# Lightning attention and an FNet block on one core: the late pairs' second layer as 49 block products instead of 7 half-size ones

## The chip, the cores and the metric

The kernel runs on one core of one Trainium2 chip. A core has a matrix engine (TensorE, in the profile PE, its weight loads PEld), a vector engine (VectorE, DVE), a scalar engine (ScalarE, ACT), a general one (GpSimd, POOL) and an engine that issues DMAs (SyncE, SP). Each takes its instructions in order from its own queue, and they wait for each other through semaphores. The metric is the device time of one execution in microseconds, as the median of several runs.

## The reference

Attention with a decaying state (4 batches, 8 heads, 768 positions, 64 wide), then an FNet block over the result, seen as x of 4 x 768 x 512. What the change touches is the last part, a two-layer network applied to each row:

```python
X = np.fft.fft(x, axis=1)
X = np.fft.fft(X, axis=2)
u = x + np.real(X)
un = (u - mean(u)) / np.sqrt(var(u) + 1e-06)
ch = np.maximum(un @ w_ch1, 0.0) @ w_ch2     # 512 -> 2048 -> 512
return u + ch
```

All data are float32.

## The kernel before

**Stages.** Attention of a batch runs by chunks of 128 positions (attn, L270 to L353), its Fourier transform and normalisation (fft_ln, L414 to L612) follow. The rows of a batch are 6 tiles of 128 x 512, taken two at a time: 12 groups (b, g), of G = 2 tiles each. The first four are PLAIN: their two layers (mlp, L636 for the first and L650 for the second) are woven into attention and transforms of later batches, so that TensorE always has something to do. The other eight are LATE. For them fft_ln writes the transposed normalised rows (utd) and the rows themselves (ud) to HBM, and after everything else they are done in four pairs by late(j), called for j = 0 to 3.

**A late pair.** One pair is a product of two matrices cut into 2 x 2 blocks, done by the Strassen-Winograd scheme: 7 block products instead of 8, on sums of blocks. The sums of weight blocks are made once, by combine_weights, part 0 before the end of the plain work and part 1 after it (w1s, w2s, and in place in w1 and w2). Late(j) first makes sums of the input blocks on DVE (L713 to L716), then the first layer: for each of HF = 8 blocks of 128 hidden columns, seven products of two matmuls each (prod, L723). ACT and DVE take the results out of PSUM, add what the scheme adds, apply the ReLU and make the sums that the second layer needs as stationary operands: h tiles named a11, a12, a22, s1, s2, s3, s4 (ha.. and hs.. in the profile). Finish(i) does the end of block i while block i+1 has begun.

The second layer (prod2, L770) runs for each of the two tiles s: seven products, each 8 matmuls of 128 x 256 that accumulate over the hidden dimension in one PSUM bank. The banks X, Y and Z are chained: the scheme's running sums are accumulated in X and Z, and DVE reads X after each step, adding the residual rows (u2, loaded by SP from ud) into the output tile y2. Store writes a tile to the output: tiles of the first half of the sequence by SP (L623), mirrored ones by an indirect DMA on GpSimd's queue (L625).

**What sets the order.** The program is written in Python generators that are woven by estimated times. The framework then orders the instructions of each engine by its own estimate, except where keep_in_program_order pins them; the order on each queue is fixed when the kernel is built. Pools reuse memory: the pools of the late part (h2, y2, p2) open when the plain ones close, on the same addresses, and "reuse_waits='tile'" makes the first use of a new tile wait for all that used its memory before.

**Memory, where it matters below.** The plain pools lie at the right-hand end of SBUF, one behind the other, per partition: x (12 tiles of 2 KB), ut (3 of 4 KB), y (one tile of 2 KB), hr (4 of 4 KB). When they are closed the pool h2 takes the same place, its tiles in the order of their first use.

Of the kernel before, what the change touches and what calls it, by code (L numbers as in the profile page):

```python
# [76 lines left out]
def kernel(  # L77
# [602 lines left out]
    def combine_weights(part):  # L680
# [16 lines left out]
        for o, x, y, op in todo:  # L697
            n = o.shape[1]
            for i in range(0, n, n // 2):
                V.tensor_tensor(o[:, i:i + n // 2], x[:, i:i + n // 2], y[:, i:i + n // 2], op=op)  # L700
                yield 1.3

    def load_u(j, queue=nc.sync):

        r = s2.u[j] = new(s2.up, [128, 2, KO, G * 128], "ur", bufs=2)
        for h, (b, g) in enumerate(LATE[2 * j:2 * j + 2]):
            queue.dma_start(r[:, h], utd[b, g])

    def late(j):
        r = s2.u.pop(j)  # L710
        b11, b21, b12, b22 = r[:, 0, 0:2], r[:, 0, 2:4], r[:, 1, 0:2], r[:, 1, 2:4]
        t = new(s2.up, [128, 3, 2, G * 128], "us")
        V.tensor_tensor(t[:, 0], b12, b11, op=SUB)  # L713
        V.tensor_tensor(t[:, 1], b22, t[:, 0], op=SUB)
        V.tensor_tensor(t[:, 2], b21, t[:, 1], op=SUB)
        V.tensor_tensor(b12, b22, b12, op=SUB)  # L716
        U = dict(b11=b11, b21=b21, b22=b22, t1=t[:, 0], t2=t[:, 1], t4=t[:, 2], t3=b12)

        h = {n: new(s2.hp, [128, G, HF, 128], f"h{n}") for n in ("a11", "a12", "a22", "s1", "s2", "s3", "s4")}
# [12 lines left out]
        def finish(i, X, Z):  # L732
            a11, a12, a22, s1, s2_, s3, s4 = (h[n][:, :, i, :] for n in ("a11", "a12", "a22", "s1", "s2", "s3", "s4"))
# [7 lines left out]
            V.tensor_tensor(s2_, s1, a11, op=SUB)  # L741
            V.tensor_tensor(s3, a11, a21, op=SUB)
            V.tensor_tensor(s4, a12, s2_, op=SUB)

        last = None
        for i in range(HF):
# [16 lines left out]
            last = (i, X, Z)  # L763
        finish(*last)
        if 2 * j + 2 < len(LATE):
            load_u(j + 1)

        def prod2(ps, a, b, s, first):
            for i in range(HF):
                nc.tensor.matmul(ps, lhsT=h[a][:, s, i, :], rhs=s2.B[b][:, i, :],  # L770
                                 start=(first and i == 0), stop=(i == HF - 1), skip_group_check=True)

        lo, hi = slice(0, HM), slice(HM, DM)
        for s in reversed(range(G)):
            who = [(b, TT[g][s]) for b, g in LATE[2 * j:2 * j + 2]]
            us, y = [], []
            for k in who:
                us.append(new(s2.yp, [128, DM], "u2", bufs=3))
                nc.sync.dma_start(us[-1], ud[k])
                y.append(new(s2.yp, [128, DM], "y2", bufs=2))  # L780
            rev = slice(DM - 1, HM - 1, -1)
            X, Y, Z = bank(), bank(), bank()
            prod2(X, "a11", "b11", s, True)
            V.tensor_tensor(y[0][:, lo], X, us[0][:, lo], op=ADD)
            prod2(Y, "a12", "b21", s, True)
            V.tensor_tensor(y[0][:, lo], Y, y[0][:, lo], op=ADD)
            prod2(X, "s2", "t2", s, False)
            V.tensor_tensor(y[1][:, lo], X, us[1][:, lo], op=ADD)
            prod2(Z, "s3", "t3", s, True)
            prod2(X, "s1", "t1", s, False)  # L790
            V.tensor_tensor(y[1][:, hi], X, us[1][:, rev], op=ADD)  # L791
            V.tensor_tensor(y[1][:, hi], Z, y[1][:, hi], op=ADD)
            if s == 0:
                store(*who[1], y[1], hi)
            prod2(X, "s4", "b22", s, False)
            V.tensor_tensor(y[0][:, hi], X, us[0][:, rev], op=ADD)  # L796
            store(*who[0], y[0])
            prod2(Z, "a22", "t4", s, False)
            V.tensor_tensor(y[1][:, lo], Z, y[1][:, lo], op=ADD)
            store(*who[1], y[1], lo if s == 0 else slice(0, DM))  # L800


# [103 lines left out]
```

## Time and profile before

| what | value |
|---|---|
| time, median of 3 runs | 822.02 us (821.09 to 824.20) |
| span of the profiled execution | 819.4 us |
| end of the plain work, start of the late pairs | 428.3 us |
| first layer of one late pair (L723) | 48.35 us |
| second layer of one late pair (L770) | 48.35 us |
| records of L770 (two for each float32 matmul) | 896 |
| last TensorE work to the end of the span | 3.5 us |
| mean granted TensorE clock | 1.000 |

The span runs from the first to the last instruction of one profiled execution; the page has no separate time for that execution, and the timed runs lie 1.7 to 4.8 us above its span. A row of the costliest groups gives a line, an engine, what is written from what, the shape, the count, busy time and mean duration of one. Two groups of GpSimd that the working below uses, from the groups by form:

```profile
L270 POOL TENSOR_TENSOR kd<-k,decay 128x512 f32<-128x512 f32 x20 | 23.0, 1152 | 94.8 <-PE pa L315 64.5 <-DMA k<-in_k_dram 16.8 <-issue 10.3
L319 POOL TENSOR_TENSOR st<-st,qpow 128x256 f32<-128x256 f32 x16 | 15.9, 996 | 34.7 <-PE pa L328 24.3 <-DVE st L320 5.3 <-PE pa L332 2.8
```

The means include waiting; the shortest are 1.06 and 0.62 us. A float32 matmul appears as two MATMUL records and two LDWEIGHTS records; [...]the distance between starts (216 ns in the second layer) is what it costs.

### The profile page before, as it was taken

Reading aid. Unit: us, or ns where it says so; the run is one execution under the profiler, and the core shown is the slowest. Engines: PE = TensorE matmul, PEld = TensorE weight load, DVE = VectorE, ACT = ScalarE, POOL = GpSimd, SP = SyncE. Lnnn points to the kernel's source line nnn. Section 1 sums busy time; section 2 is a strip of 40 time slices with the busy share of each in tenths; the row PEclk is TensorE's granted clock in tenths of the full one; section 3 lists DMA queues with packets and bytes.
Section 4 is the critical chain, followed back from the end, with each engine's and each line's share of the span. In section 5 each row is a group of like instructions: output and inputs, shape, how many; then the busy total and the mean of one; then the engine's idle time right before and its main releaser. Section 6 shows DMA issues by size and latency. Waiting matters only on the chain.

```text
span 819.4 us, 11694 instructions
## 1 busy us (share of the span) xinstructions
PE 795.2 (97%) x4608; PEld 634.9 (77%) x4608; DVE 437.8 (53%) x1018; ACT 186.5 (23%) x448; POOL 86.1 (11%) x102
## 2 busy tenths in 40 slices
PE   6989899999999999999999999999999999999998
PEld 5777767768585857768648888888888888888886
DVE  5899798766743761354895541165313661146311
ACT  3756344225420211312002200022001210022100
POOL 3223340011011010220000000000000000000000
PEclk9999999999999999999999999999999999999999
DMA  9979624248741136530351011100111001010010
GB/s 233 249 154 271 174 90 129 63 113 201 203 125 51 52 62 131 129 123 26 93 162 42 1 53 51 52 1 1 64 40 52 0 1 39 33 33 0 1 39 26
DMA packets 126684, 68.88 MB, mean 84 GB/s; under 512 B 111150, under 2 KB 112174, under 8 KB 126630
## 3 DMA queue, kind: packets, MB, share of 16 engines
q1 hardware_dynamic: 121488, 55.67, 26.6%
q0 software_dynamic: 2112, 6.69, 2.4%
q10 hardware_dynamic: 3030, 5.78, 1.9%
q8 instruction: 36, 0.59, 0.3%
q14 instruction: 18, 0.15, 0.1%
HBM read 48.72 MB, written 19.40 MB: 83 GB/s over the span
## 4 chain that ended last, share of the span: by engine, by line
PE 80%; DVE 10%; issue 4%; DMA 3%; ACT 2%; POOL 1%; POOLq 0%; ACTq 0%; DVEq 0%
PE p L770 24%; PE p L723 24%; PE pm L650 10%; PE pm L636 8%; PE pa L332 3%; PE pa L516 3%; PE pa L298 3%; DMA x<-xb,ix 2%; PE pa L328 2%; PE pa L274 1%; DVE sc L302 1%; PE pa L315 1%; PE pa L348 1%; PE pa L279 1%; DVE stt L546 1%
## 5 line engine op out<-in xcount | busy, mean ns | idle before, releaser
L636 PE MATMUL pm<-ut,w 128*128 128x256 f32 x512 | 119.2, 382 | 0.0
L650 PE MATMUL pm<-w,hr 128*128 128x512 f32 x256 | 115.8, 597 | 0.2 <-DVE w L225 0.2
L636 PEld LDWEIGHTS pm<-ut,w 128*128 128x128 f32 x512 | 94.4, 190 | 15.4 <-issue 3.6
L723 PE MATMUL p<-ur,w 128*128 128x256 f32 x384 | 93.8, 379 | 0.0
L650 PEld LDWEIGHTS pm<-w,hr 128*128 128x128 f32 x256 | 46.6, 190 | 49.5 <-issue 48.0
L723 PEld LDWEIGHTS p<-ur,w 128*128 128x128 f32 x384 | 73.0, 190 | 10.3 <-issue 0.5
L723 PE MATMUL p<-us,w1s 128*128 128x256 f32 x256 | 65.7, 379 | 0.0
L770 PE MATMUL p<-w,hs 128*128 128x256 f32 x256 | 58.0, 379 | 0.5 <-DVE y L791 0.5
L770 PE MATMUL p<-w2s,hs 128*128 128x256 f32 x256 | 57.9, 379 | 0.0
L770 PE MATMUL p<-w,ha 128*128 128x256 f32 x256 | 57.9, 379 | 0.0
L770 PEld LDWEIGHTS p<-w,hs 128*128 128x128 f32 x256 | 48.5, 190 | 7.5 <-DVE y L791 0.9
L625 POOL DMA_INDIRECT out_dram<-y,ix x12 | 11.9, 989 | 402.6 <-DVE y L796 342.6
L770 PEld LDWEIGHTS p<-w2s,hs 128*128 128x128 f32 x256 | 48.6, 190 | 6.6
L723 PEld LDWEIGHTS p<-us,w1s 128*128 128x128 f32 x256 | 48.6, 190 | 6.6
L770 PEld LDWEIGHTS p<-w,ha 128*128 128x128 f32 x256 | 48.6, 190 | 6.6
L750 ACT COPY ha<-p 128x256 f32<-128x256 f32 x32 | 11.9, 372 | 169.1 <-PE p L723 139.4
L761 DVE TENSOR_TENSOR ha<-p,ha 128x256 f32<-128x256 f32 x32 | 13.6, 424 | 45.2 <-ACT ha L760 45.2
L298 PEld LDWEIGHTS pa<-qT,kT 64*128 64x128 f32 x384 | 26.0, 193 | 13.2 <-ACT qT L281 7.3
L302 DVE TENSOR_TENSOR sc<-pa,decay 128x512 f32<-128x512 f32 x48 | 31.5, 683 | 8.8 <-PE pa L298 8.5
L332 PE MATMUL pa<-sc,v 128*64 128x128 f32 x384 | 32.1, 284 | 4.1 <-DVE sc L302 4.1
L298 PE MATMUL pa<-qT,kT 64*128 64x128 f32 x384 | 30.7, 292 | 3.2 <-ACT qT L281 2.9
L270 POOL TENSOR_TENSOR kd<-k,decay 128x512 f32<-128x512 f32 x20 | 23.0, 1152 | 94.8 <-PE pa L315 64.5
(144 smaller groups left out, 1135.0 us busy)
## 6 DMA issues: line engine op xcount, KB each, us to landing
raw<-in_moe_w_ch_dram SPq DMA_DIRECT2D x32, 512.0 KB, 4.8
k<-in_k_dram SPq DMA_DIRECT2D x24, 256.0 KB, 5.0
q<-in_q_dram SPq DMA_DIRECT2D x24, 256.0 KB, 5.9
v<-in_v_dram SPq DMA_DIRECT2D x24, 256.0 KB, 4.9
ud<-x SPq DMA_DIRECT2D x16, 256.0 KB, 2.3
utd<-e SPq DMA_DIRECT2D x64, 64.0 KB, 2.2
u<-ud SPq DMA_DIRECT2D x16, 256.0 KB, 2.7
ur<-utd SPq DMA_DIRECT2D x6, 512.0 KB, 4.3
```

The source lines that it names most:

```text
L270: nc.gpsimd.tensor_tensor(kd, kt, kpow, op=ALU.mult)
L298: mm(pss[hi][:, hp, :], lhsT=kT[HD[hi], hp, :], rhs=qT[HD[hi], hp, :], start=True, stop=True)
L302: nc.vector.tensor_tensor(t, pss[hi], decay[:, hi::2, :], op=ALU.mult)
L328: mm(po[HD[hi], hp, :], lhsT=s_old[HD[hi], hp, :], rhs=qs[HD[hi], hp, :], start=(hp == 0), stop=False, skip_group_check=True)
L332: mm(po[HD[hi], hp, :], lhsT=vt[:, 2 * hp + hi, :], rhs=sc[hi][:, hp, :], start=(c == 0 and hp == 0), stop=(hp == HP - 1), skip_group_chec ...
L516: mm = nc.tensor.matmul(ps[0:m, n, :], lhsT=piece(a, i, n), rhs=cs[0:rows, a, i in (2, 3), n, :], start=(a == 0), stop=(a == 1))
L625: nc.gpsimd.indirect_dma_start(out=out.rearrange("b s d -> (b s) d"), out_offset=row_of(2 + HC * (b + 1) + T - HC), in_=y[:, :], in_offset ...
L636: nc.tensor.matmul(ps, lhsT=w1[:, c, 128 * fc:128 * fc + 128], rhs=ut[:, c, :], start=(c == 0), stop=(c == KO - 1))
L650: nc.tensor.matmul(ps, lhsT=hr[(fc - f0) // 4][:, fc % 4, 128 * i:128 * i + 128], rhs=w2[:, fc, :], start=(fc == f0), stop=(fc == f1 - 1))
L723: nc.tensor.matmul(ps, lhsT=s2.A[a][:, kt, 128 * i:128 * i + 128], rhs=U[b][:, kt, :], start=(first and kt == 0), stop=(kt == 1), skip_gro ...
L761: V.tensor_tensor(a22, two(Z), a22, op=ADD)
L770: nc.tensor.matmul(ps, lhsT=h[a][:, s, i, :], rhs=s2.B[b][:, i, :], start=(first and i == 0), stop=(i == HF - 1), skip_group_check=True)
```

## The change

The seven block products of the second layer are each cut once more by the same scheme, into seven products of quarter blocks: 49 instead of 56. Now both tiles of a group take part (the two tiles are the row halves of the second level), so the loop over s is gone, and a matmul is 128 x 128 with 4 steps of accumulation.

- **Stationary side.** S1, S2 and S4 of a product are sums of quarters of an h tile, made on DVE (prepare_a) into tiles "sx"; the third one is made in place (split). The h tiles s2 and s4 are no longer made in the first layer: they come in the second, in place of a11 and a12, half on DVE and half on GpSimd (part_sum).
- **Moving side.** T1, T2 and T4 of a weight block are made on GpSimd for each product of each pair (prepare_b) into tiles "tx", two sets; the fourth sum is made once, in place, by seven GpSimd instructions at the end of combine_weights(1).
- **Results.** Level2 runs one product: seven groups of four matmuls, a bank read after each (give): by ACT for the first write of a fresh quarter, else by DVE, which adds. Two products are interleaved, the preparation of the next one beside them. What the outer scheme adds between outputs is done on DVE (after), the residual is added on GpSimd (add_u).
- **Tiles.** y2 now holds the whole pair, ur has one buffer instead of two, and the input sums t1, t2, t4 use the "sx" tiles.

The diff, cut:

```diff
@@ -699,24 +699,68 @@
             for i in range(0, n, n // 2):
                 V.tensor_tensor(o[:, i:i + n // 2], x[:, i:i + n // 2], y[:, i:i + n // 2], op=op)
                 yield 1.3
+        if part:
+            for b in s2.B.values():
+                q = quarters_b(b)
+                nc.gpsimd.tensor_tensor(q[1], q[3], q[1], op=SUB)
+    def quarters_a(t):
+        return [t[:, s, i:i + HF // 2] for s in range(2) for i in (0, HF // 2)]
+    def quarters_b(t):
+        return [t[:, i:i + HF // 2, m:m + HM // 2] for i in (0, HF // 2) for m in (0, HM // 2)]
 
     def load_u(j, queue=nc.sync):
 
-        r = s2.u[j] = new(s2.up, [128, 2, KO, G * 128], "ur", bufs=2)
+        r = s2.u[j] = new(s2.up, [128, 2, KO, G * 128], "ur")
         for h, (b, g) in enumerate(LATE[2 * j:2 * j + 2]):
             queue.dma_start(r[:, h], utd[b, g])
+    PRODUCTS = [("a11", "b11"), ("a12", "b21"), ("s3", "t3"), ("s2", "t2"), ("s4", "b22"), ("s1", "t1"), ("a22", "t4")]
 
     def late(j):
         r = s2.u.pop(j)
         b11, b21, b12, b22 = r[:, 0, 0:2], r[:, 0, 2:4], r[:, 1, 0:2], r[:, 1, 2:4]
-        t = new(s2.up, [128, 3, 2, G * 128], "us")
-        V.tensor_tensor(t[:, 0], b12, b11, op=SUB)
-        V.tensor_tensor(t[:, 1], b22, t[:, 0], op=SUB)
-        V.tensor_tensor(t[:, 2], b21, t[:, 1], op=SUB)
+        t1, t2, t4 = (new(s2.hp, [128, 2, G * 128], "sx", bufs=7) for _ in range(3))
+        V.tensor_tensor(t1, b12, b11, op=SUB)
+        V.tensor_tensor(t2, b22, t1, op=SUB)
+        V.tensor_tensor(t4, b21, t2, op=SUB)
         V.tensor_tensor(b12, b22, b12, op=SUB)
-        U = dict(b11=b11, b21=b21, b22=b22, t1=t[:, 0], t2=t[:, 1], t4=t[:, 2], t3=b12)
-
-        h = {n: new(s2.hp, [128, G, HF, 128], f"h{n}") for n in ("a11", "a12", "a22", "s1", "s2", "s3", "s4")}
+        U = dict(b11=b11, b21=b21, b22=b22, t1=t1, t2=t2, t4=t4, t3=b12)
+        h = {n: new(s2.hp, [128, G, HF, 128], f"h{n}") for n in ("a11", "a12", "a22", "s1", "s3")}
+        pre_a, pre_b = {}, {}
+        def split(t):
+            A11, _, A21, _ = quarters_a(t)
+            V.tensor_tensor(A21, A11, A21, op=SUB)
+        def prepare_a(k):
+            a = PRODUCTS[k][0]
+            A11, A12, A3, A22 = quarters_a(h[a])
+            S1, S2, S4 = pre_a[k] = [new(s2.hp, [128, HF // 2, 128], "sx", bufs=7) for _ in range(3)]
+            if a in ("a11", "a12", "a22", "s3"):
+                split(h[a])
+                yield 0.0
+            V.tensor_tensor(S2, A22, A3, op=SUB)
+            yield 0.0
+            V.tensor_tensor(S1, S2, A11, op=ADD)
+            yield 0.0
+            V.tensor_tensor(S4, A12, S2, op=SUB)
+            yield 0.0
+        def prepare_b(k):
+            B11, T3, B21, B22 = quarters_b(s2.B[PRODUCTS[k][1]])
+            T1, T2, T4 = pre_b[k] = [new(s2.yp, [128, HF // 2, HM // 2], "tx", bufs=6) for _ in range(3)]
+            for o, x, y, op in ((T2, T3, B11, ADD), (T1, B22, T2, SUB), (T4, B21, T2, SUB)):
+                nc.gpsimd.tensor_tensor(o, x, y, op=op)
+                yield 0.0
 
         def prod(ps, a, b, i, first):
             for kt in range(2):
@@ -730,7 +774,7 @@
             return new(s2.ps, [128, DM], "p2")[:, 0:G * 128]
 
         def finish(i, X, Z):
-            a11, a12, a22, s1, s2_, s3, s4 = (h[n][:, :, i, :] for n in ("a11", "a12", "a22", "s1", "s2", "s3", "s4"))
+            a11, a12, a22, s1, s3 = (h[n][:, :, i, :] for n in ("a11", "a12", "a22", "s1", "s3"))
             prod(X, "s4", "b22", i, False)
             a21 = new(s2.hp, [128, G, 128], "a21", bufs=2)
             nc.scalar.activation(a21, two(X), AF.Relu)
@@ -738,9 +782,7 @@
             V.tensor_tensor(a12, two(Z), a12, op=ADD)
             V.tensor_scalar(a12, a12, 0.0, None, op0=ALU.max)
             V.tensor_tensor(s1, a21, a22, op=ADD)
-            V.tensor_tensor(s2_, s1, a11, op=SUB)
             V.tensor_tensor(s3, a11, a21, op=SUB)
-            V.tensor_tensor(s4, a12, s2_, op=SUB)
 
         last = None
         for i in range(HF):
@@ -761,44 +803,132 @@
             V.tensor_tensor(a22, two(Z), a22, op=ADD)
             V.tensor_scalar(a22, a22, 0.0, None, op0=ALU.max)
             last = (i, X, Z)
+            if i == HF // 2:
+                for k in range(2):
+                    run(prepare_b(k))
+        run(prepare_a(0))
         finish(*last)
+        run(prepare_a(1))
         if 2 * j + 2 < len(LATE):
             load_u(j + 1)
 
-        def prod2(ps, a, b, s, first):
-            for i in range(HF):
-                nc.tensor.matmul(ps, lhsT=h[a][:, s, i, :], rhs=s2.B[b][:, i, :],
-                                 start=(first and i == 0), stop=(i == HF - 1), skip_group_check=True)
-
-        lo, hi = slice(0, HM), slice(HM, DM)
-        for s in reversed(range(G)):
-            who = [(b, TT[g][s]) for b, g in LATE[2 * j:2 * j + 2]]
-            us, y = [], []
-            for k in who:
-                us.append(new(s2.yp, [128, DM], "u2", bufs=3))
-                nc.sync.dma_start(us[-1], ud[k])
-                y.append(new(s2.yp, [128, DM], "y2", bufs=2))
-            rev = slice(DM - 1, HM - 1, -1)
-            X, Y, Z = bank(), bank(), bank()
...
-            prod2(Z, "a22", "t4", s, False)
-            V.tensor_tensor(y[1][:, lo], Z, y[1][:, lo], op=ADD)
-            store(*who[1], y[1], lo if s == 0 else slice(0, DM))
-
+        who = [[(b, TT[g][s]) for s in range(G)] for b, g in LATE[2 * j:2 * j + 2]]
+        us = []
+        for k in who:
+            us.append(new(s2.yp, [128, G, DM], "u2", bufs=2))
+            for s in range(G):
+                nc.sync.dma_start(us[-1][:, s], ud[k[s]])
+        yt = new(s2.yp, [128, 2, G, DM], "y2")
+        T = new(s2.yp, [128, G, HM], "t2")
+        y11, y12, y21, y22 = (yt[:, k, :, m:m + HM] for k in range(2) for m in (0, HM))
+        def add_u(k, m, y):
+            u = us[k][:, :, 0:HM] if m == 0 else us[k][:, :, DM - 1:HM - 1:-1]
+            nc.gpsimd.tensor_tensor(y, y, u, op=ADD)
+        def part_sum(o, x, y, op):
+            V.tensor_tensor(o[:, 0], x[:, 0], y[:, 0], op=op)
+            nc.gpsimd.tensor_tensor(o[:, 1], x[:, 1], y[:, 1], op=op)
+        def stores(k, cols=slice(0, DM)):
+            for s in reversed(range(G)):
+                store(*who[k][s], yt[:, k, s], cols if s == 0 else slice(0, DM))
+        def after(k):
+            if k == 0:
+                split(h["s1"])
+                h["s2"] = h["a11"]
+                part_sum(h["a11"], h["s1"], h["a11"], SUB)
+            elif k == 1:
+                V.tensor_tensor(y11, y11, T, op=ADD)
+                h["s4"] = h["a12"]
+                part_sum(h["a12"], h["a12"], h["s2"], SUB)
+                add_u(0, 0, y11)
+            elif k == 3:
+                V.tensor_tensor(y21, T, y22, op=ADD)
+                add_u(1, 0, y21)
+                add_u(1, 1, y22)
+            elif k == 4:
+                add_u(0, 1, y12)
+            elif k == 5:
+                V.tensor_tensor(y12, y12, T, op=ADD)
+                stores(0)
+                V.tensor_tensor(y22, y22, T, op=ADD)
+                store(*who[1][0], yt[:, 1, 0], slice(HM, DM))
+            elif k == 6:
+                stores(1, slice(0, HM))
+        outs = [(T, True), (y11, True), (y22, True), (T, False), (y12, True), (T, False), (y21, False)]
+        def level2(k):
+            (a, b), (y, fresh) = PRODUCTS[k], outs[k]
+            A11, A12, A3, A22 = quarters_a(h[a])
+            B11, T3, B21, B22 = quarters_b(s2.B[b])
+            (S1, S2, S4), (T1, T2, T4) = pre_a.pop(k), pre_b.pop(k)
+            X, Y, Z = (bank()[:, 0:HM // 2] for _ in range(3))
+            def prod(ps, a, b, first):
+                for i in range(HF // 2):
+                    nc.tensor.matmul(ps, lhsT=a[:, i, :], rhs=b[:, i, :], start=(first and i == 0),
+                                     stop=(i == HF // 2 - 1), skip_group_check=True)
+            def give(ps, s, m, first=False):
+                o = y[:, s, m * HM // 2:(m + 1) * HM // 2]
+                if first and fresh:
+                    nc.scalar.copy(o, ps)
+                else:
+                    V.tensor_tensor(o, ps, o, op=ADD)
+            prod(X, A11, B11, True)
+            give(X, 0, 0, True)
+            yield 0.0
+            prod(Y, A12, B21, True)
+            give(Y, 0, 0)
+            yield 0.0
+            prod(X, S2, T2, False)
+            give(X, 1, 0, True)
+            yield 0.0
+            prod(Z, A3, T3, True)
+            give(Z, 1, 1, True)
+            yield 0.0
+            prod(X, S1, T1, False)
+            give(X, 1, 1)
+            yield 0.0
+            prod(Z, A22, T4, False)
+            give(Z, 1, 0)
+            yield 0.0
+            prod(X, S4, B22, False)
+            give(X, 0, 1, True)
+            yield 0.0
+            after(k)
+        n = len(PRODUCTS)
+        live = {}
+        for at in range(7 * n + 8):
+            k = at // 7
+            if at % 7 == 0 and k < n:
+                live[k] = level2(k)
+                if k + 1 < n and k:
+                    live[-k - 1] = turns(prepare_b(k + 1), prepare_a(k + 1))
+            for q in sorted(live, key=abs):
+                if q < 0 or (at - 7 * q) % 2 == 0:
+                    if next(live[q], live) is live:
+                        del live[q]
...
```

What is left out at the end is turns(), which takes steps of two generators by turns; in the removed loop it is the five products between the first line and the last.

More of the change, by code (lines that the diff above doesn't have):

```diff
@@ L773, in late @@
-        lo, hi = slice(0, HM), slice(HM, DM)
-        for s in reversed(range(G)):
-            who = [(b, TT[g][s]) for b, g in LATE[2 * j:2 * j + 2]]
-            us, y = [], []
-            for k in who:
-                us.append(new(s2.yp, [128, DM], "u2", bufs=3))
-                nc.sync.dma_start(us[-1], ud[k])
-                y.append(new(s2.yp, [128, DM], "y2", bufs=2))
-            rev = slice(DM - 1, HM - 1, -1)
-            X, Y, Z = bank(), bank(), bank()
[L783 to L797, printed above, removed]
-            prod2(Z, "a22", "t4", s, False)
-            V.tensor_tensor(y[1][:, lo], Z, y[1][:, lo], op=ADD)
-            store(*who[1], y[1], lo if s == 0 else slice(0, DM))
@@ new lines, in late, with turns @@
+        n = len(PRODUCTS)
[10 more added lines that the diff above has]
+                        del live[q]
+    def turns(*gens):
+        gens = list(gens)
+        while gens:
+            for g in list(gens):
+                d = next(g, None)
+                if d is None:
+                    gens.remove(g)
+                else:
+                    yield d
```

## The prediction

> **What bounds the kernel now.** I read the page first, then the chain of waits, then busy time by stage, then single instructions.
>
> ```profile
> PE 795.2 (97%) x4608; PEld 634.9 (77%) x4608; DVE 437.8 (53%) x1018; ACT 186.5 (23%) x448; POOL 86.1 (11%) x102
> PE   6989899999999999999999999999999999999998
> POOL 3223340011011010220000000000000000000000
> ```
>
> TensorE is busy 97% of the span and GpSimd is empty in its second half. The chain of waits from 428.3 us on is TensorE alone:
>
> ```profile
> 428.30 46.62 PE p L723 x216
> 475.78 1.73 PE p L723 x8
> 477.51 40.58 PE p L770 x188
> 518.95 6.91 PE p L770 x32
> 525.85 45.76 PE p L723 x212
> ```
>
> L723 is the first layer of a late pair, L770 the second; four rounds follow, each half lasting 48.35 us, with no wait between. Only TensorE time counts here, unless another engine becomes late. Busy time by stage shows how idle the others are:
>
> ```profile
> 477.50:525.85 48.35, 48.35 (x226) 42.56 (x225) 9.44 (x23) 0.37 (x1) 1.92 (x2) 1.00 0.19 63
> ```
>
> (columns: window, length, busy PE, PEld, DVE, ACT, POOL.) In a second layer DVE works 9.4 us, ACT 0.4, POOL 1.9. The change spends this idleness.
>
> **The change, part by part.**
>
> **1. Fewer multiplications.** Before: 2 x 7 x 8 = 112 matmuls of 128x256 (two records each) in 48.35 us, 0.432 us each. After: 49 x 4 = 196 matmuls of 128x128. Will one cost half? The weight load stays 128x128 and shows 190 ns per record, longer than half of 216. The timeline has a dense run of this shape in the Fourier stage:
>
> ```profile
> 274.55 0.39 PE L531 MATMUL pa<-dt,ys 128*128 128x129 f32 x2
> 274.67 0.30 PEld L532 LDWEIGHTS pa<-dt,ys 128*128 128x128 f32 x2
> 274.77 0.39 PE L532 MATMUL pa<-dt,ys 128*128 128x128 f32 x2
> 275.00 0.39 PE L534 MATMUL pa<-dt,ys 128*128 128x128 f32 x2
> ```
>
> Starts are 0.222 us apart with fresh weights each time; the loads overlap. The Trainium skill, "TensorE: Matmul & The Clock Gate" (LDWEIGHTS), gives columns/1.2 ns, 107 ns for 128; twice that is 0.213, just under. So 196 x 0.222 = 43.5 us, a gain of 4.85 a pair, **19.4 in all**. Ends: 0.213 gives 41.7, 0.23 gives 45.1 us.
>
> **2. New work on DVE and GpSimd.** Within one second layer (a pair):
> - DVE, both inputs in SBUF, 128x512: 18 sums for products 1 to 6, 4 output sums, 4 of the next pair's input sums (these move into this stage): 26 at a pitch of 0.60 (0.68 long); two 1024-wide at 1.14. Together 17.9 us. 33 additions out of PSUM (128x128): the rows at 128x256 have a pitch of 0.335, so about 0.20, 6.6 us. (16 copies go to ACT, about 0.28 each by L595: covered.) DVE: 24.5 of 43.5 us. The first layer loses 16 DVE sums and gains 8; it has 48.35 - 27 us free, so nothing.
> - GpSimd: 15 block sums of 128x512 (the other 6 fall into the first layer), two of 1024, 4 residual sums. L270 (128x512) takes 1.06 when undisturbed, L319 (128x256) 0.62, so 1024 about 1.9: 15 x 1.06 + 3.9 + 4.2 = 24 us. Both rows have a broadcast operand; the Trainium skill, "GPSIMD Engine Reference" (3.1), gives 4497 ns for 2048 fp32 elements, 1.1 to 1.2 for 512. I take 1.06; 1.2 for the range.
>
> Each fits alone. Together they may not: the Trainium skill, "SBUF — State Buffer" (Who interferes with whom), says that a DVE instruction with two SBUF inputs and a GpSimd one that reads SBUF share a port and block each other wholly. The trace agrees:
>
> ```profile
> 53.92 0.68 DVE L426 TENSOR_TENSOR fe<-x,x 128x512 f32<-128x512 f32 x1
> 54.08 2.27 POOL L319 TENSOR_TENSOR st<-st,qpow 128x256 f32<-128x256 f32 x1
> 55.46 0.41 DVE L430 TENSOR_TENSOR fo<-fo 128x255 f32<-128x255 f32 x1
> ...
> 83.12 1.55 POOL L270 TENSOR_TENSOR kd<-k,decay 128x512 f32<-128x512 f32 x1 [6.20 <-PE pa L315]
> ...
> 84.00 1.21 DVE L225 SCALAR_TENSOR_TENSOR w<-w,e 128x512 f32<-128x512 f32 x1
> ```
>
> L319 waits through four DVE sums and ends 0.5 after the last; L225 takes 1.21 for 0.72, ending 0.54 after L270. So 17.9 + 24 = 42 us of port in 43.5.
>
> **3. Stalls that follow.** A PSUM bank is reused four times in a product, three group times (4 matmuls, 0.888 us) after it was written: DVE may be 2.7 us late, then TensorE stops. DVE is in order, so an addition out of PSUM stands behind each waiting sum. From the instruction order of the changed kernel (fixed when it is built), counting from the start of the second layer:
> - GpSimd can begin T4 of product 2 only when TensorE has used the buffer (8th group, 7.1). Then come the half of s2, three sums of product 3, the half of s4: 4 x 1.06 + 2 x 1.9 = 8.1, with DVE's port time between them (about 3.5) until 18.7. DVE's first sum of product 4 waits for it; behind it stand two more sums and the addition that frees product 3's bank: 18.7 + 3 x 0.65 + 0.4 = 21, wanted at 19.5: **1.5 to 1.7**. (Without contention 0.2.)
> - DVE's S2 of product 6 reuses a buffer read in group 34; behind it S1, an output sum and the addition that frees group 37's bank: 0.1 + 3 x 0.6 + 0.2 + 0.35 = 2.45 against 1.78: **0.7**.
> - The next pair's second input sum reuses a buffer read in group 41, with one more sum and an addition ahead of group 43: 1.65 against 0.89, **0.8**, to 1.2 with GpSimd on the port; absent in the last pair.
> - The last groups of product 6, with two output sums among them: **0.5**.
>
> That is 3.9 a pair, 2.9 in the last: 14.6. Ends: 1.5 a pair (6) if GpSimd slips into DVE's gaps; 6.5 a pair (26) if sums take 1.2 and the two engines alternate throughout.
>
> **4. The hand-over at 428 us.** Nothing in the diff says it, the order does. GpSimd now makes 7 in-place differences and 6 block sums, and the store of the last plain tile (y, L625), which stood alone there, comes behind these 13. The new tiles "sx" (7 x 2 KB) come first in their pool and push ha22 to 30-38 KB; y lay at 36-38 (12 x 2 KB of x, 3 x 4 KB of ut below it). So the first ACT copy into ha22 waits for that store to land. Before, y lay under s2, which is written late and no longer exists. From the timeline of before:
>
> ```profile
> 429.52 1.08 POOL L625 DMA_INDIRECT out_dram<-y,ix  x1 [25.50 <-DVE y L662]
> 432.65 0.37 ACT L760 COPY ha<-p 128x256 f32<-128x256 f32 x1 [1.35 <-PE p L723]
> 434.18 1.03 PE L723 MATMUL p<-ur,w1s 128*128 128x256 f32 x4
> ```
>
> L760 is that copy; the matmuls at 434.18 need it, and all of ACT stands behind it. On GpSimd the first two differences can run at 418 to 421; then DVE's unbroken 1024-wide sums hold the port until 426.8. From there 11 sums of 1.06 plus about 2 us lost to DVE's input sums end at 440.4; issue to landing is 3.0 (the DMA issues' median): 443.4; copy and start of the matmul 0.6: 444 instead of 434.2, **9.8**. Least: two differences need the last plain matmul (428.3): 8 sums, 3.0, 0.6 give 440.4, so 6.2. Most, at 1.2 a sum: 12. The first pair's own input sums, now behind the last plain addition, come 2 us later; inside this stall.
>
> **5. Small things.** A load of the first late pair (512 KB) moves ahead of the mirror's write on ACT's queue, and the y store ahead of the two last gathers on GpSimd: the gather comes 2 us later (y is ready at 361.5, the gather was issued at 360.8). TensorE's order has more L636 work in front of L516 now, and before waited 1.0 there: +0.3, ends 0 and 2. SP: the next pair's load waits for the first layer's end, but no store is behind it that is ready. The tail: last additions are half as wide, but an indirect store ends it too: -0.3.
>
> **Sum.** -19.4 + 14.6 + 9.8 + 0.3 - 0.3 = +5.0 on the span of 819.4, which is 2.6 under the median of the timed runs: 824.4 + 2.6 = **827**.
>
> **Rivals.**
> - Not slower (the other side): GpSimd's sums fall into DVE's gaps. GpSimd has a lead of 6 to 12 us on most tiles, which speaks for it. Stalls 1.5 a pair, hand-over 7: 822 - 19.4 + 6 + 7 = **815.5**. It decides from a stall under 2.3 a pair with the hand-over as taken.
> - The port decides: sums at 1.2, alternating; a second layer of 43.5 + 6.5 = 50. 822 - 19.4 + 26 + 12 = **841**. For it: 42 of 43.5 us of port already; against: both engines also have work without it.
> - The store does not hold ACT (the wait is met early), stalls as forecast: 822 - 19.4 + 14.6 = **817**. Against: the copy's list of waits names that store's queue event.
>
> **How the numbers follow.** Forecast 0.48 (own range 821 to 833), not slower 0.26, port 0.18, store free 0.08. About 0.5% (4.1 us) is what a measurement tells from no change: bounds 817.9 and 826.1. Faster: 0.22 from the first rival and 0.05 from the third, 0.27. Same: the forecast's lower part 0.18, the rest of those two 0.07: 0.25. Slower 0.48. For 8 in 10: 812 to 841.
>
> **What would show it.** Right: in the changed trace TensorE idle for 6 to 12 us near 434 to 444, released by ACT's copy into ha22 and a store landing near 443; second layers of 46 to 48 us; stretched sums on POOL and DVE; matmul starts 0.222 apart. Wrong: a pitch above 0.23 for 128x128 (step 1), second layers near 44 (step 3), or no idle time near 434 (step 4).

## The result and the profile after

| what | before | after |
|---|---|---|
| time, median (4 runs each, side by side) | 823.06 us | 848.38 us |
| ratio after to before, 95% interval | | 1.0313 (1.0286 to 1.0340) |
| span of the profiled execution | 819.4 us | 844.8 us |
| second layer of a late pair, first matmul to first matmul of what follows | 48.35 us | 49.3 us (49.9 with its six early records) |
| last addition to the end of the span | 3.1 us | 9.9 us |

The change makes the kernel 3.1% slower, 25.3 us. 827 was forecast, with a range up to 841. The busy times and the slices of the page, after:

```profile
PE 787.0 (93%) x5280; PEld 645.1 (76%) x5280; DVE 581.3 (69%) x1158; ACT 203.1 (24%) x512; POOL 282.2 (33%) x217
PE   7989899999999999999978998999899998999995
POOL 3223240111111101210180059800894029910593
PEclk9999999999999999999989999999999999999998
```

TensorE is busy 8 us less than before (795.2), and yet the span is longer: the busy share fell from 97 to 93%. GpSimd, empty in the second half before, now has a burst at the start of the late part and four more at 80 to 90%, one for each second layer. The clock row, all nines before, has an 8 where the late pairs begin, and one at the end.

The chain of waits in the first second layer (start, length, engine and line), which was TensorE alone before:

```profile
492.06 4.70 PE p L875 x42
496.89 3.97 POOL tx L762 x2
500.86 2.76 POOL ha L832
503.62 2.22 POOL tx L762
...
507.47 1.71 POOL tx L762
509.17 2.77 POOL ha L832
...
515.26 8.29 PE p L875 x72
```

From 497 to 512 us the chain runs over GpSimd: the path that sets the end has moved to an engine that was to work beside it. A GpSimd sum of 128x512 takes 1.6 to 2.3 us there, where the working had 1.06.

TensorE's stops in this second layer, from the timeline of its matmuls (in brackets the idle time before a group, and what ended it):

```profile
499.99 1.16 PE L875 MATMUL p<-w,sx 128*128 128x128 f32 x8 [0.56 <-DVE t L883]
508.30 1.16 PE L875 MATMUL p<-w,sx 128*128 128x128 f32 x8 [1.79 <-DVE y L883]
515.26 1.13 PE L875 MATMUL p<-tx,sx 128*128 128x128 f32 x8 [1.33 <-DVE t L883]
533.99 1.13 PE L875 MATMUL p<-tx,hs 128*128 128x128 f32 x8 [0.63 <-DVE t L883]
540.17 1.16 PE L875 MATMUL p<-w2s,sx 128*128 128x128 f32 x8 [0.45 <-DVE y L883]
```

Each is ended by L883, DVE's addition out of PSUM that frees a bank. None is ended by GpSimd directly. What stands ahead of the addition, around the longest stop:

```profile
505.91 3.26 POOL L762 TENSOR_TENSOR tx<-w2s,tx 128x512 f32<-128x512 f32 x2
506.85 1.20 DVE L752 TENSOR_TENSOR sx<-sx,ha 128x512 f32<-128x512 f32 x1 [0.47 <-PE p L875]
507.97 0.28 DVE L883 TENSOR_TENSOR y<-p,y 128x128 f32<-128x128 f32 x1
508.17 1.55 DVE L754 TENSOR_TENSOR sx<-ha,sx 128x512 f32<-128x512 f32 x1
```

The addition takes 0.28 us, but waits its turn behind sums of 1.2 to 1.7 us that take 0.68 undisturbed. Before the second line DVE also stood 0.47 us for matmuls that had to end; by the program this can be the tile sx that it writes, which is not shown. The stops with the slower restarts behind them come to 6.2 us a pair: the same groups follow each other every 0.893 us elsewhere, and 49 x 0.893 = 43.8 against 49.9, both rounded. They repeat within 0.02 us in the second and third pair; the last, without a next pair's input sums, has the first three, 4.5 us.

The hand-over from the plain work to the late pairs:

```profile
430.59 4.61 POOL L705 TENSOR_TENSOR w<-w 128x512 f32<-128x512 f32 x3 [3.43 <-DVE w L700]
434.22 2.04 PE L767 MATMUL p<-sx,w1s 128*128 128x256 f32 x4 [1.80 <-DVE sx L728]
443.77 1.08 POOL L625 DMA_INDIRECT out_dram<-y,ix  x1 [0.17 <-issue]
446.83 0.37 ACT L802 COPY ha<-p 128x256 f32<-128x256 f32 x1 [10.16 <-DMA out_dram<-y,ix]
447.26 2.08 PE L767 MATMUL p<-ur,w1s 128*128 128x256 f32 x4 [5.59 <-ACT ha L802]
```

This is the stop of step 4: the store is issued at 443.8, ACT has been held for 10.2 us when it lands, and the matmuls that stood at 434.18 stand at 447.26. Two things are new: TensorE stops for 1.80 us at 434.22, for an input sum of DVE, and its clock falls. The four records at 434.22 and at 447.26 take 2.04 and 2.08 us, where four take 1.03 elsewhere: the granted clock is 0.50 from 433.3 to 440.1 and again from 446.9 to 450.3.

The end:

```profile
832.44 1.37 POOL L625 DMA_INDIRECT out_dram<-y,ix  x1 [4.02 <-DVE y L883]
834.65 0.29 DVE L883 TENSOR_TENSOR y<-p,y 128x128 f32<-128x128 f32 x1 [0.60 <-PE p L875]
835.65 6.48 SPq L623 DMA_DIRECT2D out_dram<-y  x3
838.92 0.97 POOL L625 DMA_INDIRECT out_dram<-y,ix  x1 [5.10 <-DMA out_dram<-y]
```

The last addition is done at 834.94, the span ends at 844.8. SP's stores begin when the first indirect store has landed (832.44 + 3.16 by the chain), the second indirect store when SP's have, and the last of SP's three when that one has.

### The profile page after: what moved, and what is told of

Same layout as the page of the kernel before. It is cut to its first block, busy times and chain, and to the rows that moved or that the text cites. A ratio compares the mean times of both kernels' runs of the same rounds, so it can differ in the third digit from the quotient of the medians.

```text
span 844.8 us, 13570 instructions
## 1 busy us (share of the span) xinstructions
PE 787.0 (93%) x5280; PEld 645.1 (76%) x5280; DVE 581.3 (69%) x1158; ACT 203.1 (24%) x512; POOL 282.2 (33%) x217
## 4 chain that ended last, share of the span: by engine, by line
PE 32%; POOL 8%; DVE 7%; issue 3%; DMA 1%; POOLq 0%; DVEq 0%; ACT 0%; ACTq 0%; SPq 0%
PE p L767 22%; PE p L875 9%; POOL tx L762 5%; POOL ha L832 3%; DVE w2s L700 1%; DVE w L700 1%; DMA out_dram<-y,ix 1%; DVE w1s L700 1%; DVE ur L730 1%; DVE y L850 1%; DVE t L883 1%; POOL w L705 1%; DVE sx L754 0%; DVE sx L752 0%; DVE sx L728 0%
## 5 line engine op out<-in xcount | busy, mean ns | idle before, releaser
L762 POOL TENSOR_TENSOR tx<-w 128x512 f32<-128x512 f32 x16 | 24.7, 1546 | 182.3 <-PE p L875 182.3
L650 PEld LDWEIGHTS pm<-w,hr 128*128 128x128 f32 x256 | 46.6, 190 | 49.5 <-issue 48.0
L767 PEld LDWEIGHTS p<-ur,w 128*128 128x128 f32 x384 | 73.6, 193 | 11.9 <-PE p L767 1.3
L767 PE MATMUL p<-sx,w1s 128*128 128x256 f32 x256 | 67.6, 388 | 1.8 <-DVE sx L728 1.8
L875 PE MATMUL p<-tx,sx 128*128 128x128 f32 x448 | 59.5, 276 | 5.3 <-DVE t L883 5.3
L875 PEld LDWEIGHTS p<-tx,sx 128*128 128x128 f32 x448 | 54.5, 192 | 6.0 <-issue 6.0
L767 PEld LDWEIGHTS p<-sx,w1s 128*128 128x128 f32 x256 | 49.6, 194 | 9.1 <-issue 2.2
L270 POOL TENSOR_TENSOR kd<-k,decay 128x512 f32<-128x512 f32 x20 | 23.7, 1186 | 95.4 <-PE pa L315 53.1
L762 POOL TENSOR_TENSOR tx<-w,tx 128x512 f32<-128x512 f32 x32 | 51.1, 1619 | 4.7 <-PE p L875 4.5
L767 PE MATMUL p<-ur,w1s 128*128 128x256 f32 x128 | 34.2, 390 | 5.6 <-ACT ha L802 5.6
L762 POOL TENSOR_TENSOR tx<-w2s,tx 128x512 f32<-128x512 f32 x24 | 39.1, 1649 | 0.6
L875 PE MATMUL p<-w,ha 128*128 128x128 f32 x288 | 37.4, 275 | 0.0
L875 PEld LDWEIGHTS p<-w,ha 128*128 128x128 f32 x288 | 35.3, 192 | 0.4
```

The lines of the kernel that those rows point to most:

```text
L270: nc.gpsimd.tensor_tensor(kd, kt, kpow, op=ALU.mult)
L650: nc.tensor.matmul(ps, lhsT=hr[(fc - f0) // 4][:, fc % 4, 128 * i:128 * i + 128], rhs=w2[:, fc, :], start=(fc == f0), stop=(fc == f1 - 1))
L762: nc.gpsimd.tensor_tensor(o, x, y, op=op)
L767: nc.tensor.matmul(ps, lhsT=s2.A[a][:, kt, 128 * i:128 * i + 128], rhs=U[b][:, kt, :], start=(first and kt == 0), stop=(kt == 1), skip_gro ...
L875: nc.tensor.matmul(ps, lhsT=a[:, i, :], rhs=b[:, i, :], start=(first and i == 0), stop=(i == HF // 2 - 1), skip_group_check=True)
```

## The experiments

"Period" is the time from one pair to the next, 98.3 us in the changed kernel (96.7 before), of which 48.4 are the first layer in both. In the single executions below the late part begins between 428.0 and 432.8 us, although no edit touches what comes before it; so stages are compared rather than whole spans.

**First: another order of the stores.**

```diff
-                stores(0)
+                store(*who[0][1], yt[:, 0, 1])
                 V.tensor_tensor(y22, y22, T, op=ADD)
-                store(*who[1][0], yt[:, 1, 0], slice(HM, DM))
             elif k == 6:
-                stores(1, slice(0, HM))
+                store(*who[1][1], yt[:, 1, 1])
+                store(*who[0][0], yt[:, 0, 0])
+                store(*who[1][0], yt[:, 1, 0])
```

> Edit to the changed kernel: a pair's stores in another order (the two indirect ones for the mirrored tiles first, then the two direct ones), nothing else. Theory: the 9.9 us from the last addition (834.94) to the end (844.8) are a chain of writes to the same output that wait for each other: indirect (landed 835.6), direct (838.9), indirect (841.7), direct. With both indirect stores ahead the chain is indirect, indirect, direct: landed about 835.6, 838.6, 840.7, then 1.3 to the end, so the tail falls by about 3 us to 6.5 to 7, and all else stays. Rival: the tail is the cost of issuing the indirect stores themselves, or of the slower 128-wide ends: then it stays within 1 us of 9.9.

One execution: span 843.3, and 8.4 us from the last addition (834.9) to the end. The indirect stores are issued at 832.4 and 836.6, the direct ones at 839.5. The gain is 1.5 us, half of what was expected: the second indirect store is issued 4.2 us after the first and lands at 839.4, where 838.6 was expected, and the last direct one lands at 842.2, where 840.7 was. This neither settles the chain nor rules it out; the seventh experiment goes on from here.

**Second: the place of the tiles.**

```diff
+        h = {n: new(s2.hp, [128, G, HF, 128], f"h{n}") for n in ("a11", "a12", "a22")}
         t1, t2, t4 = (new(s2.hp, [128, 2, G * 128], "sx", bufs=7) for _ in range(3))
...
-        h = {n: new(s2.hp, [128, G, HF, 128], f"h{n}") for n in ("a11", "a12", "a22", "s1", "s3")}
+        h.update({n: new(s2.hp, [128, G, HF, 128], f"h{n}") for n in ("s1", "s3")})
```

> Edit to the changed kernel: the tiles a11, a12, a22 of the hidden layer are requested before the tiles sx, so that the last plain tile y lies under an sx tile that is first written near the second layer, and not under a22. No instruction is added or removed. Theory (step 4 of the prediction): TensorE's stop of 5.6 us record to record at 447.3 is ACT waiting for the store of y behind the 13 sums of GpSimd; it goes, and matmuls that stood at 447.3 stand at 435 to 438 (some wait for the input sums remains, since GpSimd's differences still take the port). Span shorter by 9 to 12 us. Rival: the stop has a second cause close behind (the slowed DVE sums or the banks): shorter by under 4 us.

One execution: span 835.2, 9.6 us shorter. Lines are one further down here (L768 is the first layer). The stops at the hand-over:

```profile
433.26 2.04 PE L768 MATMUL p<-sx,w1s 128*128 128x256 f32 x4 [1.80 <-DVE sx L729]
439.24 1.03 PE L768 MATMUL p<-ur,w1s 128*128 128x256 f32 x4
```

The second is the group that stood at 447.26; it has no wait any more, and stands 8 us earlier (435 to 438 was expected). Of the 9.6 us, 1.0 is the start of the late part, at 428.4 here and 429.4 in the changed kernel, so a tile's place in memory was worth 8.6 us, with no instruction added or removed. Step 4's mechanism is shown. The stop of 1.80 us and the half clock behind it remain.

**Third: without the weights' block sums.**

```diff
-            T1, T2, T4 = pre_b[k] = [new(s2.yp, [128, HF // 2, HM // 2], "tx", bufs=6) for _ in range(3)]
-            for o, x, y, op in ((T2, T3, B11, ADD), (T1, B22, T2, SUB), (T4, B21, T2, SUB)):
-                nc.gpsimd.tensor_tensor(o, x, y, op=op)
+            pre_b[k] = [B11, B21, B22]
+            for _ in range(3):
                 yield 0.0
```

> Edit to the changed kernel: the block sums T1, T2, T4 of the second layer's weights are left out; the products read the weight blocks themselves in their place. That leaves out 84 sums of 128x512 on GpSimd; TensorE and DVE do all that they did. Theory (GpSimd and DVE take the shared port from each other, and DVE's additions out of PSUM stand behind the stretched sums): DVE's sums return to about 0.68 us from 0.92 to 1.66, and the stops of TensorE in a second layer fall from 6.2 us to 1 to 2; the second layer from 49.95 to about 45. The stop at the hand-over falls too, since 6 of the 13 sums ahead of the store are gone. Span 844.8 - 3 x 4.7 - 3.5 - 7 = 820. Rival (DVE's own queue and the buffers that it waits for): stops stay at 4 us or more a pair.

One execution: span 811.5. The second pair's second layer, without its six early records, by busy time (columns as in the prediction), and two groups of DVE's sums in the whole kernel:

```profile
573.70:616.80 43.10, 43.10 (x388) 43.10 (x386) 30.42 (x64) 4.27 (x16) 12.38 (x7) 1.00 0.14 51
```

```profile
L752 DVE TENSOR_TENSOR sx<-sx,ha 128x512 f32<-128x512 f32 x20 | 13.7, 687 | 1.2 <-PE p L874 0.5
L752 DVE TENSOR_TENSOR sx<-sx,hs 128x512 f32<-128x512 f32 x8 | 5.5, 690 | 0.4
```

TensorE is busy for all of 43.10 us: no stop is left, not even the 1 to 2 us that the theory had kept. The same window in the changed kernel, and the same groups:

```profile
590.24:639.50 49.26, 44.48 (x388) 43.55 (x387) 44.12 (x64) 4.25 (x16) 43.73 (x25) 1.00 0.13 44
```

```profile
L752 DVE TENSOR_TENSOR sx<-sx,ha 128x512 f32<-128x512 f32 x20 | 19.1, 956 | 0.8 <-PE p L875 0.5
L752 DVE TENSOR_TENSOR sx<-sx,hs 128x512 f32<-128x512 f32 x8 | 13.3, 1661 | 0.4
```

DVE executes the same 64 instructions in both; they take 30.4 us beside 7 instructions of GpSimd (12.4 us) and 44.1 beside 25 (43.7). That difference, 13.7 us, is what the 18 further sums of GpSimd cost DVE; that it comes about at the shared port is the prediction's reading. So the order of DVE's queue and its buffers alone, the rival, stop nothing.

**Fourth: the halves of s2 and s4 on DVE.**

```diff
             V.tensor_tensor(o[:, 0], x[:, 0], y[:, 0], op=op)
-            nc.gpsimd.tensor_tensor(o[:, 1], x[:, 1], y[:, 1], op=op)
+            V.tensor_tensor(o[:, 1], x[:, 1], y[:, 1], op=op)
```

> Edit to the changed kernel: the halves of the sums s2 and s4 that GpSimd makes (128x1024, 2.8 us each, one of each per pair) are made by DVE too. Theory of the port: GpSimd loses 5.6 us a pair, DVE gains 2 x 1.2; the two largest stops (1.79 and 1.33 between records, released by DVE behind these halves) shrink by half or more; the second layer goes from 49.95 to 48 or less. Rival (DVE is the queue that is too long): DVE has 2.4 us more, and the second layer stays or grows by 1 to 2.

One execution: span 852.1; 3.4 us of it arose before the late part, which no edit touches, so the pairs are compared. The period is 99.1 us against 98.3: the rival's number. Of the two stops that were to shrink, that of 1.33 us is gone and that of 1.79 is longer; that of 0.63 us has become 1.06.

```profile
513.13 1.20 PE L875 MATMUL p<-w,sx 128*128 128x128 f32 x8 [2.04 <-DVE y L883]
514.13 1.91 PE L875 MATMUL p<-w,hs 128*128 128x128 f32 x8
```

Behind it the granted clock is 0.50 for 3.4 us (514.1 to 517.5): eight records take 1.91 us instead of 1.06, which costs 1.7 us a pair. Without that the second layer would be about 48.3 us, where the changed kernel has 49.3: one us less, and two were expected. My expectation had left out what a stop itself brings after it; it failed, and the experiment doesn't part the two theories cleanly.

**Fifth: the sums made once, kept in HBM.** With the edits of the first two, the seven in-place differences moved from combine_weights to the first pair's first layer, and

```diff
-            if i == HF // 2:
+            if j == 0 and i:
+                k = (i + 1) % len(PRODUCTS)
+                q = quarters_b(s2.B[PRODUCTS[k][1]])
+                nc.gpsimd.tensor_tensor(q[1], q[3], q[1], op=SUB)
+                run(prepare_b(k, True))
+            elif j and i == HF // 2:
                 for k in range(2):
                     run(prepare_b(k))
...
+                if make:
+                    nc.gpsimd.tensor_tensor(o, x, y, op=op)
+                    s2.td[k, n] = dram.tile([128, HF // 2, HM // 2], F32, name=f"td{k}{n}")
+                    nc.sync.dma_start(s2.td[k, n], o)
+                else:
+                    nc.sync.dma_start(o, s2.td[k, n])
```

> The changed kernel with the tile order and the store order of the first two experiments, and with the block sums T1, T2, T4 made once: GpSimd makes all 21 in the first layer of the first pair (each with the in-place difference of its block), SP writes them to HBM, and every later product loads its three by DMA into the same buffers; nothing is left out. Theory (the sums on GpSimd beside DVE's sums in the second layer cause the stops): second layers of 43 to 44 us in all four pairs; span about 811.5 (run without the sums) less 1.5 for the stores, plus 0 to 4 for the stretched first layer of pair 0: 808 to 815, a time of 811 to 818, under the kernel before. Rival: loads that come late (256 KB took 2.3 to 5 us, behind other entries on SP's queue) put new stops into the products, 1 us or more each: 820 or more.

819.3 us against 822.46 of the kernel before, ratio 0.9967 (0.9950 to 0.9985). No second layer has a stop; the loads are always in time. So the 49 products pay, if only by 3 us, once their sums leave the port. The span, 816.0, is at the wrong side of 815, above all because the first pair's first layer stops now, for 2.50, 0.40 and 0.41 us:

```profile
445.48 4.50 DVE L785 TENSOR_SCALAR ha<-ha 128x256 f32<-128x256 f32 x1
446.11 2.50 POOL L760 TENSOR_TENSOR tx<-w,tx 128x512 f32<-128x512 f32 x2
...
450.37 1.13 PE L769 MATMUL p<-sx,w 128*128 128x256 f32 x4 [2.50 <-DVE ha L805]
```

A ReLU on DVE, one input, 0.29 us alone, is held off for 4.50 us by GpSimd's unbroken run of sums, until a pause of 0.08 us in it at 449.81; the addition L805 behind it frees TensorE.

**Sixth: the other side of the port, without DVE's sums.**

```diff
-            S1, S2, S4 = pre_a[k] = [new(s2.hp, [128, HF // 2, 128], "sx", bufs=7) for _ in range(3)]
...
+            pre_a[k] = [A11, A12, A22]
```

with the four DVE sums behind them left out.

> Edit to the changed kernel: DVE's sums S1, S2, S4 and the in-place differences of a product's stationary operand are left out, the quarters themselves are used (20 of DVE's 512-wide sums a pair go); GpSimd makes all its sums as before. Theory of the port that only one of the two holds at a time: GpSimd's sums fall from 1.55 to 1.9 us to about 1.25 (as they are where DVE stands still, at 439.8), and the stops of the second layer fall to under 1 us. Rival (GpSimd is simply this slow, and its products come late): its sums stay at 1.5 or more, and TensorE stops for T1, T2, T4.

One execution: span 824.2. GpSimd has all its sums, and the stops of a second layer are one of 0.2 us in each of the first three pairs; with the slower restarts a second layer there is 0.7 to 1.2 us over the 43.8 without a stop. A group of its sums, here and then in the changed kernel:

```profile
L755 POOL TENSOR_TENSOR tx<-w,tx 128x512 f32<-128x512 f32 x32 | 42.4, 1343 | 7.1 <-PE p L868 6.9
```

```profile
L762 POOL TENSOR_TENSOR tx<-w,tx 128x512 f32<-128x512 f32 x32 | 51.1, 1619 | 4.7 <-PE p L875 4.5
```

The sums fall from 1.62 to 1.34 us here (1.34 to 1.63 over the four groups), not quite to the 1.25 that was expected. GpSimd is thus not simply too slow: taking either engine's sums away ends the stops or all but ends them, and only both together are too much.

**Seventh: direct stores only.**

```diff
-                store(*who[k][s], yt[:, k, s], cols if s == 0 else slice(0, DM))
+                b, t = who[k][s]
+                c = cols if s == 0 else slice(0, DM)
+                nc.sync.dma_start(out[b, 128 * t:128 * t + 128, c], yt[:, k, s][:, c])
```

> Edit to the changed kernel: the late pairs' mirrored tiles are stored by direct DMAs too (their rows not mirrored), so that no store goes to rows that the program can't name. Theory of the tail (indirect and direct stores wait for each other to land): no store waits for another, and from the last addition to the end of the span it takes 3 to 4 us instead of 9.9, as in the kernel before (3.1). Rival (the first experiment gave only 1.4 of the 3 us expected: the stores themselves are long): 7 us or more remain.

One execution: span 838.6; the last addition is done at 835.5, so the end takes 3.1 us, as in the kernel before. So 6.8 us go with the indirect stores. That they are the waiting of one kind of store for the other is read from the lines on the end above; this run has no indirect store at all, and doesn't part the waiting from what such a store takes by itself.

**Eighth: the differences pinned behind the store.** In the fifth kernel,

```diff
-                nc.gpsimd.tensor_tensor(q[1], q[3], q[1], op=SUB)
+                tc.keep_in_program_order(nc.gpsimd.tensor_tensor(q[1], q[3], q[1], op=SUB))
```

> As the fifth experiment, with the seven in-place differences pinned behind the store of the last plain tile on GpSimd's queue, each ahead of its block's sums. Theory: the stops of 1.80 and 0.48 us at the hand-over are DVE's input sums stretched by these differences (1.3 to 1.75 us each instead of 0.68); they go, with the half clock that follows them (433 to 440): matmuls that stood at 440.8 stand at 436 to 437; span 3 to 4.5 us under 816.0, less what the fuller first layer gives back (28 sums in it now: up to 2 us). Rival: the stop at the hand-over is the order of DVE's queue, input sums behind the last plain addition; then they stay.

816.74 us, ratio to the kernel before 0.9928 (0.9907 to 0.9949). The stops of 1.80 and 0.48 us are 0.22 and 0.89, with no half clock there, and the group that stood at 440.8 in the fifth kernel stands at 437.6, about as expected (436 to 437). But the profiled span, 815.3, gains only 0.7: a new stop in the fuller first layer takes the rest.

```profile
464.03 3.26 POOL L760 TENSOR_TENSOR tx<-w,tx 128x512 f32<-128x512 f32 x2
464.42 1.74 DVE L737 TENSOR_TENSOR hs<-hs 128x512 f32<-128x512 f32 x1
466.09 0.41 DVE L805 TENSOR_TENSOR ha<-p,ha 128x256 f32<-128x256 f32 x1
...
466.55 2.08 PE L769 MATMUL p<-sx,w 128*128 128x256 f32 x4 [3.73 <-DVE ha L805]
```

**Ninth: the first pair's ReLUs on ACT,** in the eighth kernel:

```diff
+        def relu(a):
+            if j == 0:
+                nc.scalar.activation(a, a, AF.Relu)
```

> As the eighth, with the ReLU of a11, a12, a22 of the first pair on ACT and no longer on DVE (24 instructions of 128x256 in place). Theory: the stops of 2.50, 0.40 and 0.41 us in the first layer of the first pair came from such a ReLU on DVE that GpSimd's sums held off (4.50 us for 0.29); on ACT they don't meet GpSimd, and the stops go: 2 to 4 us under the eighth. Rival: ACT's queue, which also copies out of PSUM, becomes late in its turn: no gain, or slower.

823.36 us, ratio 1.0005 (0.9993 to 1.0017): the rival. An ACT ReLU waits for DVE's addition, and ACT's next copy out of PSUM waits behind it; TensorE stops 1.66 us for that copy in each of three blocks and 0.82 in another, and once 2.86 for DVE.

**Tenth: DVE's early differences back in their place,** in the eighth kernel:

```diff
-            V.tensor_tensor(A21, A11, A21, op=SUB)
+            op = V.tensor_tensor(A21, A11, A21, op=SUB)
+            if j == 0:
+                tc.keep_in_program_order(op)
```

> As the eighth, with the first pair's in-place differences of the stationary operands on DVE pinned in their place in the program (before, three of them ran in a block in the middle of the first layer, 1.4 to 1.75 us each beside GpSimd's sums, ahead of an addition that TensorE waited 3.73 us for). Theory: that stop and the half clock after it (465 to 471.5) go: 4 to 6 us under the eighth, a time of 811 to 813. Rival: the pinned differences come late in the second layer in their turn and stop TensorE there: within 1.5 us of the eighth.

812.62 us, ratio to the kernel before 0.9881 (0.9852 to 0.9909), span 810.1. The stop of 3.73 us is gone; what came back later is one of 0.64 us at 500.9. This is what was expected (811 to 813). It is the fastest version, 1.2% under the kernel before, with all of its 49 products.

## Why the prediction was wrong

The sign of the likeliest case was right, the size was not: 25 us were lost where it had 5. Two terms were mis-sized above all, the stops in the second layers (8.5 us short, by way of the price of a GpSimd sum in step 2) and the tail (7.0 us short). By its own steps, on the span:

| step | predicted | measured | shown by |
|---|---|---|---|
| 1, 49 products | -19.4 | 4 x (43.8 - 48.35) = -18.2 | third: 43.1 us + 0.67 for the early records, no stop |
| 3, stops in the second layers | +14.6 | 3 x 6.2 + 4.5 = +23.1 | third, sixth |
| 4, hand-over | +9.8 | +11.9, and +1.6 for the half clock behind it | second |
| 5, front | +0.3 | +1.2 | scatter: with the same front the late part began at 428.0 us in the first experiment, 0.1 ahead of the kernel before |
| 5, tail | -0.3 | +6.7 | first, seventh |
| sum | +5.0 | +26.3 (25.4 measured) | |

The remaining 0.9 us are for the most part in the row of step 1: in the kernel before, the last pair's second layer took 0.8 us longer than the 48.35 that stands there for it.

**Step 1 held.** Starts are 0.2233 us apart (0.893 for a group of four), 0.222 was taken from the Fourier stage.

**Step 2 is where it failed first**, in one term: 1.06 us for a GpSimd sum of 128x512. That was L270, a multiplication whose second operand is broadcast. The sums of this change add or subtract two full tiles, and where DVE stands still they take 1.26 us:

```profile
439.77 1.26 POOL L762 TENSOR_TENSOR tx<-w 128x512 f32<-128x512 f32 x1
441.12 2.48 POOL L762 TENSOR_TENSOR tx<-w,tx 128x512 f32<-128x512 f32 x2
```

The end that I had kept for the range, 1.2, was the better value. It was an estimate from the Trainium skill's "GPSIMD Engine Reference" (3.1), which gives 4497 ns for 2048 fp32 elements, so 1.12 for 512; the trace has 1.26, and that counts. The broadcast row was nearer in shape but not in what it reads; whether the broadcast or the operation makes it cheaper is not shown. The halves of 1024 took 2.8 us in the changed kernel, and 2.35 at the least in the third and sixth experiments, not 1.9. With 1.26 and 2.4, the port in a second layer is asked for 19 x 1.26 + 2 x 2.4 = 28.7 us by GpSimd and 17.9 by DVE, an estimate: 46.6 of 43.5 us, where the prediction had 42. A sum just under the limit was taken to leave 3.9 us of stops a pair; it was just over. This budget doesn't give the size of the stops, though: in the fourth experiment the same estimate gives 44.1, and the stops with their restarts were still 5.2 us a pair without the half clock.

**Step 3** had the mechanism: DVE's additions out of PSUM behind stretched sums, which the third and sixth experiments show from both sides. Of its four stops, two came where they were put: 0.8 at the next pair's input sums (0.63 between records, 0.88 with the slower restart), 0.5 in the last groups (0.45, 0.80). That at product 3 was 1.5 (1.33 and 1.57), and it is the wait that was named there, DVE's first sum of product 4 for GpSimd's half of s4:

```profile
511.97 1.74 DVE L750 TENSOR_TENSOR sx<-ha 128x512 f32<-128x512 f32 x1 [1.85 <-POOL ha L832]
```

The one at product 6 for want of a buffer didn't come, and two came that weren't seen, 0.83 and 2.07, both while GpSimd makes the sums of products 2 and 3. That these two come from the mis-sized term is argued, not shown: no run varies the price alone. With 6.5 us a pair as its upper end, worked out with sums of 1.2, the rival "the port decides" was the right case, and had 0.18.

**Step 4** was right in place, cause and order, and 2 us short: the sums ended at 443.6 instead of 440.4, 1.2 of which is the later start. Four of the 13, not two, ran ahead of the last DVE sums of 1024, but these took up to 2.28 us beside them, where they took 1.22 before, so the other nine began only at 430.6; they took 1.26 to 1.71 us each. The half clock afterwards was not in the working. The Trainium skill, "TensorE: Matmul & The Clock Gate" (Part 1), says that the clock falls to half after an idle window of some 3.4 us and recovers after one of work; this trace agrees where it shows 3.4 us at 0.50 from the end of the stop of 5.59 us on, but it also shows 6.8 us that began within the second of two smaller stops, of 0.93 and 1.80, and there the measurement counts.

**Step 5, the tail, is the second failure.** "An indirect store ends it too" was not true: in the kernel before, the mirrored tiles (s = 1) are done first, and the last indirect store is issued at 794.6, more than 20 us ahead of the end. In the changed kernel both rows of a pair end together, so indirect and direct stores meet at the end, and each kind waits for the other. The trace of before had the hint: that store stood 4.6 us for the one before it to land.

The port rival's 841 with 6.7 for the tail gives 847, near the measured 848. That it is so near is in part luck: its stops of 26 us were 23.1, and it had no half clock. The parts but the tail and the clock were there, and the wrong case was taken for the likeliest.

## What to carry to other kernels

Add up the time on a port that two engines share, with each sum priced as it will read (two full tiles, no broadcast), before calling either engine idle; where it comes near the length of the stage (46.6 us of 43.5 here, an estimate), go through what stands behind those sums in an in-order queue. Where a value is made again in each round and the DMA queues are idle, make it once and load it. When a change moves work to a round's end, or asks for tiles in another order, go through who waits for whom there: a store behind other work, and an output tile's writes that wait for each other, cost some 9 and 7 us here.

## What was not expected of the hardware

- Short stops cost more than themselves. A stop of 2.04 us was followed by 3.4 us at a granted clock of 0.50, 1.7 us more; stops of 1.79 us in the same stage were not. The idle window of about 3.4 us that the skill's page names was not reached in one piece. Nor is the length of a stop enough: one of 2.50 us in the fifth experiment had no half clock behind it. In each trace the half clock begins at points that lie whole multiples of 3.41 us apart, and lasts one or two such steps, the very end left out. With the late parts of the changed kernel and of all ten experiments cut at these points, TensorE's idle time within one piece nearly tells them apart: the clock was halved behind all 18 pieces with 1.98 us of it or more, and behind none with up to 1.84 that ran at full clock, but for one of 1.78. The stop of 2.50 us fell into two pieces, with 1.42 and 1.08.
- A GpSimd run of sums held DVE off for several of them: 4.50 us for a single-input ReLU of 0.29. The Trainium skill, "SBUF — State Buffer" (Who interferes with whom), names tensor_scalar in its two-port modes among those that take the shared pair; the prediction had counted only sums with two inputs.
